# Gated linear attention and a routed two-layer network on one core: batches in pairs with both states in PSUM, padded tile loads, rows of x in 64x64 products, weights loaded later, steps in another order

## The chip, the cores and the metric

One core of a Trainium2 chip. The time is device microseconds of one launch. The core's engines run beside each other: TensorE (PE; the loading of its weights is shown as PEld), VectorE (DVE), ScalarE (ACT), GpSimd (POOL), and SyncE (SP), which here only starts transfers. 16 DMA engines carry all transfers.

## What is computed

Inputs q, k, v and alpha have 4 batches, 8 heads, 768 steps and 48 values per head. Per batch and head a 48x48 state runs through time:

```python
for t in range(S):
    state = alpha[:, :, t, :, None] * state + np.einsum('bhd,bhe->bhde', k[:, :, t], v[:, :, t])
    y[:, :, t] = np.einsum('bhd,bhde->bhe', q[:, :, t], state)
```

The result, as 3072 rows x of 384 values, goes into a routed network: rows with `x @ w_skip > 0` are computed, each by the one of 8 experts with the largest logit `x @ w_gate`:

```python
h = np.maximum(xc[mask] @ w1[e], 0.0)          # 384 -> 1024
y[mask] = gate_w[mask, None] * (h @ w2[e])     # 1024 -> 384
out[do_compute] = xc + y
```

All other rows are copied. Everything is fp32.

## The kernel before

**Tiles.** A tile i is 128 time steps of one batch with all 8 heads; there are 24 (`NT`). Heads lie in pairs, 48 of 64 partitions each. Tiles go through the four batches in turn: tiles 0 to 3 are the first 128 steps of batches 0 to 3, so that a batch comes back four tiles later, and each batch has its state in SBUF (`state`, four buffers).

**One tile.** `load` (L200) brings the decays, k and q (`qka`, 1551 columns) and v. Tiles 0 and 1 come from `first`, an array padded to 128 partitions, in three pieces; the later ones in two transfers of 48 partitions, moved by 16 partitions in odd tiles (`shift`), into one of six buffers that were filled with zeros at the start. `decay` (L215) makes running products of alpha: a forward scan `pfx` on DVE (L219) and a reciprocal, POOL multiplies q by it (L222); a backward scan `sfx` on DVE (L224), and POOL multiplies k by that (L226). PE then makes `scores` (L229) in 64x64 quadrants of its array, and DVE's `causal` (L240) copies their lower triangle out of PSUM. `turn_k` (L244) turns k with four full-array transposes, and ACT copies the result (`kt`, L252). The state: `held` (L256) puts the old state into PSUM with a product with the identity (L259), `outer` (L262) adds the products of k and v of the two halves of the tile (s = 0 and 1, L272) with a copy of the state between them (`half`, L276), and `carry` (L278) multiplies by the tile's total decay while it copies the state to SBUF (L281). y is summed in PSUM from `inter` (query times state) and `intra` (scores times v), both L290, and copied by `turn_y` (L328). One iteration later `rows` (L331) turns y into rows of x together with the logits, in four products (8 records) that use 112 of the 128 array rows and 105 columns (L335), into bank `pg`; `row_copy` (L341) takes x out on ACT, `logits` (L346) sums the logits on DVE, `store` writes the 128 rows to the output.

**Order.** All orders are written by hand in `static_path`: the queue of each engine is the order of the calls. In iteration i of the loop (L824 to L901): load(i+5), store(i-2), a quarter of a weight matrix, scores(i+1), causal(i+1), inter(i), outer(i,1), carry(i), intra(i,0), turn_k(i+2), rows(i-1), decay(i+3), intra(i,1), turn_y(i), held(i+1), outer(i+1,0), row_copy(i-1), logits(i-1). `tick` spreads the routing operations of finished groups of tiles (groups of 6, 6, 6, 3, 2, 1) over the iterations; `rank`, `place`, `one_hot` and `table` give each row its slot in its expert's list. `weight_splits` cuts the weights into a high part (ACT) and a remainder (POOL or DVE), a sixth of a matrix at a time. `follow` adds a wait by hand.

**Weights.** `weight_loads` (L502) goes through w1 and w2 of expert 0, then 1 and so on, four transfers of 384 KB per matrix, into three buffers. 16 of these transfers are issued in the loop (i = 3 to 14 and 19 to 22), the rest by `advance(loads, 4)` after each expert's `up` and after its `down`.

**End of the loop and experts.** After the loop the last tiles are routed and the rows of expert 0 are gathered by products (`late_rows`) into three PSUM banks `x0t`. Then, for each expert: `up` (L584), `turn` of the next expert's gathered rows, `down` (L606) and a scatter. `guard` loads alpha once more in eight pieces through one buffer and lets ACT look for values out of range, to take a slower general path if need be.

Of the kernel before, what the change touches and what calls it, by code (L numbers as in the profile page):

```python
# [29 lines left out]
NF = 2  # L30
N = B * S
# [16 lines left out]
RW = 2 * D + E + 1  # L48
GO = NP * RW
# [11 lines left out]
class Kernel:  # L61
    def __init__(self, ctx, tc, first, qka, v, w9, w1, w2, nat, w9n, out):
        self.ctx, self.tc, self.nc = ctx, tc, tc.nc
        self.qka, self.v, self.w9, self.w1, self.w2, self.out = qka, v, w9, w1, w2, out
        self.first, self.nat, self.w9n = first, nat, w9n
        self.scatters = {}

    @staticmethod
    def row(i):
        return i % B * S + i // B * P  # L70

    @staticmethod
    def shift(i):
        return 16 * (i % 2)
# [35 lines left out]
    def attention_pools(self, st):  # L110
# [10 lines left out]
        self.state = [fix.tile([P, NP, D], F32, name=f"state{b}") for b in range(B)]  # L121
# [7 lines left out]
    def early_constants(self):  # L129
        nc, const = self.nc, self.const  # L130
        zero = nc.const_aps.tensor(0.0, [P, 1], F32)
# [19 lines left out]
    def row_constants(self):  # L151
# [4 lines left out]
        for h in range(2):  # L156
            r = slice(64 * h, 64 * h + D)
            nc.sync.dma_start(out=self.xw[r, :, 2 * D:], in_=self.w9[h])
            nc.scalar.copy(out=self.xw[r, :, h * D:(h + 1) * D],
                           in_=self.ident[r, r].unsqueeze(1).to_broadcast([D, NP, D]))  # L160
# [19 lines left out]
    def slot_constants(self):  # L180
# [10 lines left out]
        nc.gpsimd.iota(iv[:, :, 0:1].rearrange("p (c b) w -> p c b w", b=B), pattern=[[P, C], [S, B], [0, 1]],  # L191
                       base=-OFF, channel_multiplier=0)
# [7 lines left out]
    def load(self, i):  # L200
        nc = self.nc
        t = self.qkab[i % NQ]
        if i < NF:
            for s in (slice(0, DEC), slice(KO, QO), slice(QO, QW)):
                nc.sync.dma_start(out=t[:, s], in_=self.first[i, :, s])
        else:
            for r in range(2):
                o = HP * r + self.shift(i)
                nc.sync.dma_start(out=t[o:o + D, :], in_=self.qka[i - NF, r])
# [3 lines left out]
                            kh=t[:, KO:QO].rearrange("p (a t) -> p a t", t=P))  # L213

    def decay(self, i, eng=None):  # L215
        nc, w = self.nc, self.work[i]
        dec = w["dec"]
        pfx = self.sc.tile([P, DEC + 1], F32, name="pfx", bufs=5)
        nc.vector.tensor_tensor_scan(pfx[:, 0:DEC], dec, self.floor.to_broadcast([P, DEC]), FLOOR, ALU.mult, ALU.max)  # L219
        nc.vector.reciprocal(dec[:, P + 1::SEG], pfx[:, P + 1::SEG])  # L220
        w["total"] = pfx.rearrange("p (a w) -> p a w", w=SEG)[:, :, P + 2:P + 3]
        nc.gpsimd.tensor_tensor(w["qh"], w["qh"], pfx.rearrange("p (a w) -> p a w", w=SEG)[:, :, 1:P + 1], ALU.mult)  # L222
# [33 lines left out]
    def held(self, i):  # L256
        if i >= NT or i < B:
            return
        self.nc.tensor.matmul(self.pv[:, 0:NP * D], lhsT=self.ident, rhs=self.state[i % B].rearrange("p a d -> p (a d)"),  # L259
                              start=True, stop=True, skip_group_check=True)  # L260

    def outer(self, i, s):  # L262
        if i >= NT or (s == 1 and i // B == C - 1):
            return
        w = self.work[i]
        t = slice(HP * s, HP * (s + 1))
        pv = self.pv[:, 0:NP * D].rearrange("p (a d) -> p a d", d=D)
        for p in range(NP):
            for r in range(2):
                h = 2 * p + (r ^ p % 2)  # L270
                a = slice(HP * r, HP * (r + 1))
                self.nc.tensor.matmul(pv[a, p, :], lhsT=w["kt"][t, p, a], rhs=w["v"][t, h * D:(h + 1) * D],  # L272
                                      start=(i < B and s == 0 and p == 0), stop=True, skip_group_check=True)
# [4 lines left out]
    def carry(self, i):  # L278
        if i // B == C - 1:
            return  # L280
# [745 lines left out]
```

## Time and profile before

| | us |
|---|---|
| median of 3 runs | 336.9 |
| lowest and highest run | 336.19, 338.39 |
| the profiled execution | 336.32 |
| its span, first to last instruction | 334.5 |

PE is busy 286.5 us of the span, DVE 191.8, POOL 190.2, ACT 149.0. The attention loop ends at about 166 us of the span, the experts begin at about 182. Busy times overlap; a stage's bound is read from what waits for what in it. Records of PE are passes: an fp32 product shows as two records.

### The profile page before, as it was taken

The page shows a single profiled execution, that of the slowest core. Times are in us where ns is not written, and L with a number is a line of the kernel's source. Part 1 is how long each engine was busy: PE and PEld are TensorE (multiplying, and loading weights), DVE is VectorE, ACT ScalarE, POOL GpSimd, SP SyncE. Part 2 cuts the span into 40 slices and gives each one's busy share as a digit, 9 for nine tenths or more (in the row PEclk, how much of TensorE's full clock was granted, in tenths as well). Part 3 has the DMA queues.
Part 4 walks back from the last instruction along what each step waited for, and adds up shares of the span by engine and source line. Part 5 has one row for each costly group of instructions (what it writes and reads, how often), then busy time and mean ns, then how long its engine had stood idle before and what let it go on. Part 6 is the DMA issues. An engine that isn't in the chain of part 4 may idle for free.

```text
span 334.5 us, 10415 instructions
## 1 busy us (share of the span) xinstructions
PE 286.5 (86%) x4384; PEld 267.7 (80%) x4384; DVE 191.8 (57%) x368; ACT 149.0 (45%) x300; POOL 190.2 (57%) x208
## 2 busy tenths in 40 slices
PE   1767998787999888988897699998979899999991
PEld 1557987676878786877797599998979799999991
DVE  7564667683377846775054823819367386656540
ACT  6112233331234432352313636939396795555410
POOL 4543373373577749581495675746646487655521
PEclk9965699996599979998569979999999999999997
DMA  7999699989799985234110174958859496842100
GB/s 245 189 191 220 164 238 278 238 174 205 193 289 248 264 185 152 74 97 122 53 48 4 43 256 159 361 174 294 299 209 328 148 340 221 292 131 92 34 21 23
DMA packets 25495, 61.01 MB, mean 182 GB/s; under 512 B 4118, under 2 KB 11183, under 8 KB 25440
## 3 DMA queue, kind: packets, MB, share of 16 engines
q1 hardware_dynamic: 23264, 55.22, 58.8%
q0 software_dynamic: 2176, 5.05, 4.4%
q8 instruction: 36, 0.59, 0.8%
q14 instruction: 19, 0.16, 0.2%
HBM read 52.63 MB, written 8.85 MB: 184 GB/s over the span
## 4 chain that ended last, share of the span: by engine, by line
PE 53%; DMA 11%; ACT 11%; issue 9%; DVE 8%; POOL 5%; SPq 2%; POOLq 0%; ACTq 0%; DVEq 0%
PE ps_o L615 10%; PE ps_h L599 9%; PE ps_y L290 8%; DMA alpha<-in_nat_dram 8%; PE ps_g L335 6%; PE ps_v L272 6%; ACT over L568 4%; PE ps_k L250 3%; PE ps_v L259 3%; PE ps_s L237 3%; DMA qka<-in_qka_dram 3%; ACT w2h L531 2%; POOL qka L226 2%; DVE pfx L219 2%; SPq L511 1%
## 5 line engine op out<-in xcount | busy, mean ns | idle before, releaser
L222 POOL TENSOR_TENSOR qka<-qka,pfx 128x512 f32<-128x512 f32 x24 | 26.2, 1092 | 53.4 <-DVE pfx L219 17.6
L615 PE MATMUL ps_o<-w2h,hh 128*112 128x384 f32 (+1 forms) x128 | 44.2, 346 | 0.0
L615 PE MATMUL ps_o<-w2l,hh 128*112 128x384 f32 (+1 forms) x128 | 43.9, 343 | 0.0
L615 PE MATMUL ps_o<-w2h,hl 128*112 128x384 f32 (+1 forms) x128 | 43.7, 341 | 0.0
L535 POOL TENSOR_TENSOR w2l<-raw,w2h 128x512 fp32r<-128x512 f32 x18 | 24.2, 1346 | 28.3 <-ACT w2h L531 28.3
L272 PEld LDWEIGHTS ps_v<-vt,kt 64*64 64x64 f32 x704 | 30.7, 162 | 11.0 <-issue 7.9
L272 PE MATMUL ps_v<-vt,kt 64*64 64x48 f32 x704 | 35.4, 247 | 4.4 <-issue 3.7
L599 PE MATMUL ps_h<-xh,w1h 128*128 128x240 f32 x192 | 32.9, 277 | 6.4 <-DVE hl L604 4.8
L252 ACT COPY kt<-ps_k 128x512 f32<-128x512 f32 x24 | 14.0, 584 | 49.6 <-PE ps_k L250 49.6
L604 DVE SCALAR_TENSOR_TENSOR hl<-ps_h,hh 128x480 fp32r<-128x480 f32 x32 | 20.8, 650 | 26.3 <-ACT hh L603 26.2
L535 POOL TENSOR_TENSOR w1l<-raw,w1h 128x512 fp32r<-128x512 f32 x24 | 31.4, 1310 | 4.5 <-ACT w1h L531 4.3
L226 POOL TENSOR_TENSOR qka<-qka,sfx 128x512 f32<-128x512 f32 x23 | 29.3, 1273 | 7.6 <-DVE sfx L224 6.7
L290 PE MATMUL ps_y<-st,vt 64*48 64x64 f32 x768 | 29.6, 250 | 4.6 <-issue 3.5
L599 PEld LDWEIGHTS ps_h<-xh,w1h 128*128 128x128 f32 x192 | 27.3, 190 | 7.2 <-DVE hl L604 5.3
L620 POOL DMA_INDIRECT out_dram<-o,ids x16 | 18.7, 1168 | 24.4 <-DVE o L618 22.2
L219 DVE TENSOR_TENSOR_SCAN pfx<-qka,ps_c 128x527 f32<-128x527 f32 x24 | 29.8, 1240 | 4.6 <-DMA qka<-in_qka_dram 3.8
L599 PE MATMUL ps_h<-xh,w1l 128*128 128x240 f32 x192 | 32.4, 275 | 0.0
L237 PE MATMUL ps_s<-qka 64*64 64x64 f32 x768 | 22.9, 255 | 10.6 <-DVE qka L226 7.2
L599 PE MATMUL ps_h<-xl,w1h 128*128 128x240 f32 x192 | 31.7, 274 | 0.0
L224 DVE TENSOR_TENSOR_SCAN sfx<-qka,ps_c 128x525 f32<-128x525 f32 x24 | 29.9, 1247 | 2.7 <-POOL slots L198 0.5
L568 ACT ACTIVATE over<-alpha,lim 128x1152 bf16<-128x1152 f32 x16 | 20.2, 1264 | 24.0 <-DMA alpha<-in_nat_dram 23.7
L453 POOL DMA_INDIRECT xr<-out_dram,ids x18 | 21.2, 1178 | 14.5 <-DVE gate L385 8.7
(139 smaller groups left out, 666.1 us busy)
## 6 DMA issues: line engine op xcount, KB each, us to landing
raw<-in_w_dram SPq DMA_DIRECT2D x64, 384.0 KB
qka<-in_qka_dram SPq DMA_DIRECT2D x44, 290.8 KB
vt<-in_v_dram SPq DMA_DIRECT2D x24, 192.0 KB
out_dram<-x SPq DMA_DIRECT2D x24, 192.0 KB
alpha<-in_nat_dram SPq DMA_DIRECT2D x8, 576.0 KB
out_dram<-xr SPq DMA_DIRECT2D x6, 192.0 KB
qka<-in_first_dram SPq DMA_DIRECT2D x4, 256.0 KB
qka<-in_first_dram SPq DMA_DIRECT2D x2, 263.5 KB
```

Source lines behind the costliest of these rows:

```text
L219: nc.vector.tensor_tensor_scan(pfx[:, 0:DEC], dec, self.floor.to_broadcast([P, DEC]), FLOOR, ALU.mult, ALU.max)
L222: nc.gpsimd.tensor_tensor(w["qh"], w["qh"], pfx.rearrange("p (a w) -> p a w", w=SEG)[:, :, 1:P + 1], ALU.mult)
L224: nc.vector.tensor_tensor_scan(sfx[:, 2:DEC][:, ::-1], dec[:, 2:DEC][:, ::-1], self.floor.to_broadcast([P, DEC - 2]), FLOOR, ALU.mult, ALU ...
L226: (eng or nc.gpsimd).tensor_tensor(w["kh"], w["kh"], sfx.rearrange("p (a w) -> p a w", w=SEG)[:, :, 2:P + 2], ALU.mult)
L237: self.nc.tensor.matmul(self.ps[t, r, p * HP:(p + 1) * HP], lhsT=kh[a, p, t], rhs=qh[a, p, t], start=True, stop=True, skip_group_check=True)
L272: self.nc.tensor.matmul(pv[a, p, :], lhsT=w["kt"][t, p, a], rhs=w["v"][t, h * D:(h + 1) * D], start=(i < B and s == 0 and p == 0), stop=Tr ...
L290: return self.nc.tensor.matmul(self.py[HP * c:HP * c + D, p % 2, o:o + HP], lhsT=lhsT, rhs=rhs, start=first, stop=True, skip_group_check=True)
L453: return [self.nc.gpsimd.indirect_dma_start(out=xr[:n, j, :], out_offset=None, in_=self.out[:, :], in_offset=bass.IndirectOffsetOnAxis(ap= ...
L535: eng.tensor_tensor(lo[:, s], raw[:, s], hi[:, s].bitcast(F32), ALU.subtract)
L568: nc.scalar.activation(out=over, in_=a, func=AF.Relu, scale=scale, bias=self.lim[:, j:j + 1], accum_out=self.odd[:, j, g:g + 1])
L599: nc.tensor.matmul(ps[:, u, :], lhsT=a[:, k, f * P:(f + 1) * P], rhs=b[:, k, :], start=(n == 0), stop=(n == len(order) - 1))
L615: nc.tensor.matmul(ps[:r], lhsT=a[:, f, js], rhs=b[:, f, :], start=(n == 0), stop=(n == 3 * FT - 1))
```

## The change

- **Pairs.** Tiles go through two batches at a time (`G = 2`): tiles 0 to 11 are batches 0 and 1, tiles 12 to 23 batches 2 and 3. Both states stay in one PSUM bank (`region`). `held` is gone; `carry` multiplies in place in PSUM; a new `keep` lets ACT copy the state to SBUF for the next `inter`. `outer` waits for the last `carry`.
- **Loads.** All tiles are padded to 128 partitions on the host and loaded in one transfer (tiles 0 and 1 in three pieces, as before). The zero fills, `first` and `shift` are gone. Tile 5 is loaded before the loop, ahead of the small loads of `xw`.
- **Rows.** `rows` makes 16 products per tile in 64x64 quadrants, 48 rows by 57 columns, into the two banks of the scores, columns 256 on; `row_copy` and `logits` read these two banks.
- **Order.** `decay` is called in two parts: the forward scan after `carry`, the backward scan after `row_copy` and `logits`, which now follow `rows` at once. `outer(i+1, 0)` comes before `intra(i, 1)`.
- **Weights.** 12 quarters are issued in the loop, one each at i = 5, 8, 10, 12 and two each at i = 18 to 21; splits start at i = 10 instead of 6. The late clears move from i = 10..15 to i = 15..20.

```diff
+G = 2
-RW = 2 * D + E + 1
-GO = NP * RW
+RW = D + E + 1
+RO = NP * HP
+GO = 0
...
+    def chunk(i):
+        return i % (G * C) // G
...
     def row(i):
-        return i % B * S + i // B * P
+        return (i // (G * C) * G + i % G) * S + Kernel.chunk(i) * P
...
-        nc.vector.memset(self.qkab[2], 0.0)
-        for i in range(3, 5):
-            nc.scalar.copy(out=self.qkab[i], in_=zero.to_broadcast([P, QW]))
...
     def load(self, i):
-        if i < NF:
-            for s in (slice(0, DEC), slice(KO, QO), slice(QO, QW)):
-                nc.sync.dma_start(out=t[:, s], in_=self.first[i, :, s])
-        else:
-            for r in range(2):
-                o = HP * r + self.shift(i)
-                nc.sync.dma_start(out=t[o:o + D, :], in_=self.qka[i - NF, r])
+        for s in (slice(0, DEC), slice(KO, QO), slice(QO, QW)) if i < NF else (slice(0, QW),):
+            nc.sync.dma_start(out=t[:, s], in_=self.qka[i, :, s])
...
-    def held(self, i):
-        if i >= NT or i < B:
-            return
-        self.nc.tensor.matmul(self.pv[:, 0:NP * D], lhsT=self.ident, rhs=self.state[i % B].rearrange("p a d -> p (a d)"),
-                              start=True, stop=True, skip_group_check=True)
...
     def outer(self, i, s):
-        pv = self.pv[:, 0:NP * D].rearrange("p (a d) -> p a d", d=D)
+        pv = self.region[i % G]
...
+                if s == p == r == 0 and self.carried:
+                    self.follow(ins.ins, self.carried)
...
     def carry(self, i):
-        self.nc.vector.tensor_tensor(self.state[i % B], self.pv[:, 0:NP * D].rearrange("p (a d) -> p a d", d=D),
-                                     self.work[i]["total"].to_broadcast([P, NP, D]), ALU.mult)
+        pv = self.region[i % G]
+        ins = self.nc.vector.tensor_tensor(pv, pv, self.work[i]["total"].to_broadcast([P, NP, D]), ALU.mult)
+        self.carried = ins.ins.name
+
+    def keep(self, i):
+        self.nc.scalar.copy(out=self.state[i % G], in_=self.region[i % G])
...
     def rows(self, i):
         for p in range(NP):
-            self.nc.tensor.matmul(bank[:, p * RW:(p + 1) * RW], lhsT=w["xt"][:PD, p, :], rhs=self.xw[:PD, p, :],
-                                  start=True, stop=True, skip_group_check=True)
+            for s in range(2):
+                for c in range(2):
+                    a = slice(HP * c, HP * c + D)
+                    t = slice(HP * s, HP * (s + 1))
+                    self.nc.tensor.matmul(self.ps[t, c, RO + p * RW:RO + (p + 1) * RW], lhsT=w["xt"][a, p, t],
+                                          rhs=self.xw[a, p, :], start=True, stop=True, skip_group_check=True)
...
-            for i in range(1, 5):
+            for i in range(1, 6):
                 self.load(i)
...
-                if i + 5 < NT:
+                if 0 < i < NT - 5:
                     self.load(i + 5)
...
-                if 3 <= i < 15 or 19 <= i < 23:
+                if i in (5, 8, 10, 12):
                     advance(loads)
-                if 10 <= i < 16:
-                    self.clear_late(i + 8)
+                if 18 <= i < 22:
+                    advance(loads, 2)
+                if 15 <= i < 21:
+                    self.clear_late(i + 3)
...
                 self.carry(i)
-                tick(2)
+                tick(1)
+                if i + 3 < NT:
+                    self.decay(i + 3, 0)
                 self.intra(i, 0)
...
                 if i:
                     self.rows(i - 1)
+                    self.row_copy(i - 1)
+                    self.logits(i - 1)
                 if i + 3 < NT:
-                    self.decay(i + 3)
+                    self.decay(i + 3, 1)
+                if not last:
+                    self.outer(i + 1, 0)
                 self.intra(i, 1)
                 self.turn_y(i)
+                self.keep(i)
                 if last:
                     break
-                self.held(i + 1)
-                self.outer(i + 1, 0)
-                if i:
-                    self.row_copy(i - 1)
-                    self.logits(i - 1)
...
-                if 6 <= i < 18:
+                if 10 <= i < 22:
                     advance(splits)
...
-            self.x0t = [self.ps[:, 0, 0:ROOM], self.ps[:, 1, 0:ROOM], self.pk[:, 0:ROOM]]
+            self.x0t = [self.pk[:, 0:ROOM], self.pv[:, 0:ROOM], self.py[:, 0, 0:ROOM]]
```

## Rows read from the trace of the kernel before

**Rows 1.** Busy time by stretch; the first line names the columns.
```profile
core 0: us, PE busy (x) PEld busy (x) DVE busy (x) ACT busy (x) POOL busy (x), PEclk, DMA share, GB/s
...
4.00:9.00 5.00, 1.78 (x36) 1.69 (x36) 4.54 (x7) 2.18 (x4) 1.94 (x3) 1.00 1.07 318
...
20.00:30.00 10.00, 9.47 (x206) 8.86 (x199) 5.14 (x8) 3.24 (x8) 4.88 (x8) 0.50 1.07 200
40.00:75.00 35.00, 29.91 (x866) 26.34 (x864) 25.84 (x49) 13.18 (x29) 19.45 (x30) 1.00 0.95 233
77.40:91.10 13.70, 13.26 (x272) 11.55 (x268) 4.97 (x10) 3.67 (x8) 5.55 (x6) 0.51 0.78 176
```

**Rows 2.** ACT's order of time: start, us, then the copy in `turn_y`, L328.
```profile
20.49 0.58 ACT L328 COPY xt<-ps_y 112x512 f32<-112x512 f32 x1 [0.80 <-PE ps_y L290]
...
41.77 0.58 ACT L328 COPY xt<-ps_y 112x512 f32<-112x512 f32 x1 [0.74 <-PE ps_y L290]
...
166.09 0.58 ACT L328 COPY xt<-ps_y 112x512 f32<-112x512 f32 x1 [2.32 <-PE ps_y L290]
```

**Rows 3.** Chain that ended last, 40 to 62 us: start, us, what.
```profile
39.82 0.59 PE ps_k L250 x4
...
42.77 0.42 PE ps_s L237 x25
...
44.36 0.59 PE ps_k L250 x4
44.95 0.87 PE ps_g L335 x8
...
46.20 0.52 PE ps_v L259 x2
```

**Rows 4.** The same chain, its longest pieces over the whole span.
```profile
5.04 9.13 DMA qka<-in_qka_dram
...
17.09 1.28 POOL qka L226
18.41 0.67 PE ps_k L250 x4
...
74.68 2.50 issue
...
79.82 0.77 PE ps_s L237 x28
...
84.59 1.67 PE ps_g L335 x8
...
86.87 0.94 PE ps_v L259 x2
...
88.83 0.77 PE ps_s L237 x28
```

**Rows 5.** Waits of the whole span: us in total, times, longest us.
```profile
DVE ps_c L346 <- ACT x L341: 42.9, 22, 4.9
...
ACT over L568 <- DMA alpha<-in_nat_dram: 23.7, 4, 8.6
...
PE ps_y L290 <- issue: 6.1, 7, 2.5
...
PE ps_h L599 <- DVE hl L604: 4.8, 3, 2.0
...
PE ps_v L272 <- issue: 3.7, 2, 1.9
...
PE ps_s L237 <- issue: 3.4, 2, 2.3
```

**Rows 6.** Groups by line: count, busy us, mean ns, idle before.
```profile
L224 DVE TENSOR_TENSOR_SCAN sfx<-qka,ps_c 128x525 f32<-128x525 f32 x24 | 29.9, 1247 | 2.7 <-POOL slots L198 0.5
...
L341 ACT COPY x<-ps_g 128x384 f32<-128x384 f32 x23 | 11.2, 485 | 0.0
...
L346 DVE TENSOR_REDUCE ps_c<-ps_g 128x9 f32<-128x36 f32 x23 | 4.7, 204 | 43.1 <-ACT x L341 42.9
```

More of the change, by code (lines that the diff above doesn't have):

```diff
@@ L120, in attention_pools @@
         self.stb = [fix.tile([P, 2, NP * HP], F32, name=f"st{i}") for i in range(2)]
-        self.state = [fix.tile([P, NP, D], F32, name=f"state{b}") for b in range(B)]
+        self.state = [fix.tile([P, NP, D], F32, name=f"state{b}") for b in range(G)]
+        self.region = [self.pv[:, b * NP * D:(b + 1) * NP * D].rearrange("p (a d) -> p a d", d=D) for b in range(G)]
         self.xtb = [fix.tile([P, NP, P], F32, name=f"xt{i}") for i in range(2)]
@@ L157, in row_constants @@
             r = slice(64 * h, 64 * h + D)
-            nc.sync.dma_start(out=self.xw[r, :, 2 * D:], in_=self.w9[h])
-            nc.scalar.copy(out=self.xw[r, :, h * D:(h + 1) * D],
+            nc.sync.dma_start(out=self.xw[r, :, D:], in_=self.w9[h])
+            nc.scalar.copy(out=self.xw[r, :, 0:D],
                            in_=self.ident[r, r].unsqueeze(1).to_broadcast([D, NP, D]))
@@ L212, in load, with decay @@
         self.work[i] = dict(dec=t[:, 0:DEC], v=vt, qh=t[:, QO:QW].rearrange("p (a t) -> p a t", t=P),
-                            kh=t[:, KO:QO].rearrange("p (a t) -> p a t", t=P))
-    def decay(self, i, eng=None):
+                            kh=t[:, KO:QO].rearrange("p (a t) -> p a t", t=P), begun=set())
+    def decay(self, i, part, eng=None):
         nc, w = self.nc, self.work[i]
         dec = w["dec"]
[L218 to L222, printed above, removed]
+        if part == 0:
+            pfx = self.sc.tile([P, DEC + 1], F32, name="pfx", bufs=5)
+            nc.vector.tensor_tensor_scan(pfx[:, 0:DEC], dec, self.floor.to_broadcast([P, DEC]), FLOOR, ALU.mult,
+                                         ALU.max)
+            nc.vector.reciprocal(dec[:, P + 1::SEG], pfx[:, P + 1::SEG])
+            w["total"] = pfx.rearrange("p (a w) -> p a w", w=SEG)[:, :, P + 2:P + 3]
+            nc.gpsimd.tensor_tensor(w["qh"], w["qh"], pfx.rearrange("p (a w) -> p a w", w=SEG)[:, :, 1:P + 1],
+                                    ALU.mult)
+            return
         sfx = self.sc.tile([P, DEC + 1], F32, name="sfx")
@@ L295, in inter @@
         for s in range(2):
-            if not s and i < B:
+            if not s and self.chunk(i) == 0:
                 continue
-            src = w["half"] if s else self.state[i % B]
+            src = w["half"] if s else self.state[i % G]
             for p in range(NP):
@@ L913, in static_path @@
             self.late_split(a)
-            self.rows(b, bank=self.pv)
-            self.logits(b, bank=self.pv)
-            self.row_copy(b, bank=self.pv)
+            self.rows(b)
+            self.logits(b)
+            self.row_copy(b)
             last = self.route(groups[5], nc.vector)
@@ L970, in static_path @@
                 advance(loads, 4)
-NAMES = ("first", "qka", "v", "w9", "w1", "w2", "nat", "w9n")
+NAMES = ("qka", "v", "w9", "w1", "w2", "nat", "w9n")
 def kernel_body(tc, *args):
@@ L993, in layouts @@
     flat = lambda a: a.reshape(NT, 2, D, -1)
-    qka = np.concatenate([flat(decay)[..., :DEC], flat(heads(k)), flat(heads(q))], axis=3)
-    first = np.zeros((NF, P, QW), qka.dtype)
-    for i in range(NF):
-        for r in range(2):
-            o = HP * r + Kernel.shift(i)
-            first[i, o:o + D] = qka[i, r]
-    qka = qka[NF:]
-    vt = v.reshape(B, H, C, P, D).transpose(2, 0, 3, 1, 4).reshape(NT, P, DM)
+    qka = np.zeros((NT, 2, HP, QW), alpha.dtype)
+    qka[:, :, :D] = np.concatenate([flat(decay)[..., :DEC], flat(heads(k)), flat(heads(q))], axis=3)
+    qka = qka.reshape(NT, P, QW)
+    vt = tiles(v).transpose(0, 2, 1, 3).reshape(NT, P, DM)
     w9 = np.concatenate([moe_w_gate, moe_w_skip[:, None]], axis=1).reshape(NP, 2, D, E + 1).transpose(1, 2, 0, 3)
@@ L1007, in layouts @@
     w2 = moe_w2.reshape(E, FT, P, DM).transpose(0, 2, 1, 3).reshape(E, P, FT * DM)
-    return [np.ascontiguousarray(a) for a in (first, qka, vt, w9, w1, w2, nat, w9n)]
+    return [np.ascontiguousarray(a) for a in (qka, vt, w9, w1, w2, nat, w9n)]
 def kernel(**inputs):
```

63 lines of the change are left out of this document (31 added, 32 removed).

## The prediction

> **What bounds the kernel now.** I read first the table by stretch of time, then the chain of work that ended last, then groups by line, then the waits. TensorE (PE) is the engine that is nearly always busy, at two clock levels: 0.50 of full speed in 20 to 30 us, 1.00 in 40 to 75 us, 0.51 in 77.4 to 91.1 us [rows 1]. The attention loop has 24 iterations, one per tile; the copy of the finished tile (`turn_y`, L328) marks each: tile 0 at 20.49, tile 3 at 41.77, tile 23 at 166.09 [rows 2]. So the 20 iterations after tile 3 take 124.3 us, 6.2 each. How long is a clean one? In the chain at full clock, one `turn_k` starts at 39.82 and the next at 44.36: 4.54 us, all PE [rows 3]. At the lower level the scores start at 79.82 and again at 88.83: 9.01 us [rows 4]. The rest of 124.3: 20 x 4.54 = 90.8; "issue" waits of PE 13.2 in eleven [rows 5], of which some 10.8 fall here, the longest 2.50 [rows 4]; about three low-clock iterations at 4.47 extra, 13.4; what is left, 9.3, I put on routing work. DMA shows a busy share of 1.07 in 20 to 30 us and 0.95 in 40 to 75 us [rows 1].
>
> **Part 1, state kept in PSUM.** `held` goes: an identity product of 2 records in 20 tiles, 0.52 us at full clock [rows 3], 0.94 at the lower [rows 4], all on PE's chain. `carry` stays one VectorE (DVE) operation of the same shape, now written to PSUM; `keep` adds an ACT copy of 192 columns, under the 0.485 us of the 384-column copy [rows 6], on an engine that is busy 13.2 of 35 us [rows 1]. Hidden by that; uncovered it would be 20 x 0.49 = 9.8 us at most. The new wait, `outer(i+1,0)` behind `carry(i)`, has `intra`, `turn_k` and `rows` in front of it on PE, over 1.1 us [rows 3]; cost between 0 and the length of a late carry; I take 0.
>
> **Part 2, rows of x in quadrants.** 8 records become 32. At full clock the 8 take 0.87 us [rows 3]. Score products have the same quadrant form: 25 records in 0.42 us, 16.8 ns each [rows 3], so 32 take 0.54: -0.33. At the lower level 1.67 becomes 32 x 0.77/28 = 0.88: -0.79 [rows 4]. The bounds are 0 (no gain) and these. With part 1, PE needs 4.54 - 0.52 - 0.33 = 3.69 us per clean iteration, and 9.01 - 0.94 - 0.79 = 7.28 at the lower level.
> The Trainium skill (TensorE: Matmul & The Clock Gate, "Wait — 56ns, not 53.3ns?") states that start to start never falls below about 25 ns. By that the rows would take 0.80, an estimate, and the sum below would end 5 us later; the trace's 16.8 ns differs, and it decides here.
>
> **Part 3, the order of steps.** This puts the gain of PE in doubt. `decay` is cut: its forward scan comes right after `carry`, its backward scan behind `row_copy` and `logits` of tile i-1. So a ring closes: `turn_k(i+2)` 0.59, `rows` 0.54, row copy 0.49, `logits` 0.20, backward scan 1.25, POOL's product for k 1.28, then `turn_k(i+3)` [rows 3, 4, 6]. The hand-off from POOL to PE took 0.04 (17.09 + 1.28 to 18.41 [rows 4]); for five I allow 0.25. Sum 4.60. PE has 0.9 us to spare per iteration, and 4.6, not 3.69, is the pace at full clock. At the lower level PE's 7.28 is the longer.
> `logits` waited for the row copy 22 times, 42.9 us [rows 5]: two readers of one bank follow each other. The Trainium skill (PSUM — Partial Sum Buffer, Terms) has it as a rule that two engines must not read one bank at once; the trace agrees. If the new layout let them overlap, the ring would be 4.1 and the sum 10 us less.
> The rows now lie in the banks of the scores, so `scores(i+2)` also waits for that copy and sum. These end about 0.7 us after `rows`, beside `outer` and `intra`; I take 0, with 0.5 per iteration as the other end.
>
> **Part 4, one padded load per tile.** 596 KB in two transfers of 48 partitions become 794 KB over 128. Which rate? In 4 to 9 us, when the padded tiles 0 and 1 were loaded over 128 partitions, DMA moved 318 GB/s; in 20 to 30 us, with 48-partition loads, 200 GB/s at a full busy share [rows 1]. So 2.5 us per tile at the one rate and 4.0 at the other, against 3.0 now. I take 2.5, the row of the same shape. Tile 2 sets the start: PE's `turn_k(2)` waits until 18.41 for a chain that begins with its load, a DMA piece of 9.13 us to 14.17 [rows 4]. 1.98 MB before it and its 0.794 MB at 318 GB/s are 8.7 us, from about 2: 10.7, and 3.3 us (rounded) come off the start (at 200 GB/s it is 1.0 later). The zero fills that go stood beside DMA waits: 0. The small load of `xw` is moved behind tile 5: 5.9 MB ahead of it, 18.7 us at 318 GB/s, so it lands near 21, when `rows(0)` is due near 20; with its latency I charge 2 us (0 to 12).
>
> **Part 5, weights later.** 12 quarters rather than 16 are loaded in the loop, 4 of them before iteration 13; the first split moves four iterations later, and its POOL products lie beside PE as now. In the expert stage each matrix is loaded one place later. ScalarE waits there four times for the guard's alpha, 23.7 us, and PE three times behind it, 4.8 us [rows 5]: now SP stands before a weight load until the splits free a buffer, and alpha is behind it. After the change the first load finds a free buffer and alpha g0 comes early; later ones trade places with loads that land just in time. Bounds -4.8 and, one matrix of 1.57 MB late at 233 GB/s [rows 1], +7. I take -1.5. The last tile's rows at the end of the loop, at the lower level, give -0.8.
>
> **Sum.** Start -3.3. Iterations 1 to 3 have no `held` now: rows 3 x 0.79 = -2.4 against `xw` +2, so about 0. The 20 iterations: 20 x 4.60 = 92.0; issue waits, those parts over PE's 0.9 spare: 5; low clock in 2.5 iterations x (7.28 - 4.60) = 6.7; routing 8 of 9.3, as a little is covered by the spare: 111.7 against 124.3, -12.6. With -0.8 and -1.5: -18.2. The profiled execution took 336.3 us (its span 334.5 and 1.8 around it): 318.1. The median shown is 336.9, 0.2% above; 318 is my time for either.
>
> **Rivals.**
> 1. The split `decay` costs more: POOL also makes one-hots and weight remainders between two k products, and if they stand in front of it the ring is 5.2, 20 x 0.6 = +12: 330. For: every link of the ring is a wait. Against: POOL is busy only 19.5 of 35 us [rows 1].
> 2. The padded third is paid at today's rate. After the first tiles 27.9 MB must move before tile 23 can be scanned (22 tiles of 0.991, 18 stores and 5 clears of 0.197, 4 weight quarters of 0.39). At 200 GB/s 140 us: tile 23 lands near 148; it is scanned in iteration 20, so some 3.4 iterations of 6.2 are left and the loop ends at 169: +3, less 2.3 of tail and experts: 337. From 235 GB/s on it lands before 128 and is hidden. For: 200 is the rate of unmixed tile loads. Against: their 48 partitions.
> 3. Slower: the clock. PE's full-array work (`held`, 128-wide `rows`) gives way to small products and idle time in the ring; if PE then runs at its lower level for 12 of the 20 iterations rather than 2.5, 9.5 x 2.68 = +25: 343. It decides from 9 iterations on (then nothing is gained). For: at 0.51 PE stayed 13.7 us though busy 13.3 of them. Against: at 29.9 busy of 35 us it kept 1.00 [rows 1].
> 4. The expert stage loses all three waits and the low-clock stretches vanish: -3.3 and -5 more, 310.
>
> **Chances.** Forecast 0.62 (309 to 327), rival 1 0.14, rival 2 0.07, rival 3 0.07, rival 4 0.10. A measurement tells about 1%, 3.4 us, from no change. Faster by over 1%: forecast and rivals 1 and 4, 0.86; within: rival 2, 0.07; slower: rival 3, 0.07. The range 303 to 332 leaves out rivals 2 and 3 and a little at either end.
>
> **What would show it.** Tile 2's forward scan before 11.5 us; DMA over 260 GB/s in 5 to 20 us; clean iterations of 4.5 to 4.8 with a short PE wait for POOL's k product; 32 records of rows in under 0.6 us; granted clock 1.00 in most of 40 to 140 us; `turn_y` of tile 23 near 149; the expert stage within 2 us of before. Wrong if iterations stay above 5.5 at full clock, if the scans wait for loads in the loop, or if the clock is low in half of it.

## The result: 4.9% faster, with most of the gain at the start

The changed kernel took 323.07 us (median of 4 runs, 318.52 to 324.42) beside 337.64 us for the kernel before on the same chip (4 runs, 336.19 to 346.26): a ratio of 0.951, 95% interval 0.935 to 0.967. The forecast was 318.0 with a range of 303 to 332. The profiled execution took 324.42 us, its span 322.6. Executions of one kernel differ by 2 to 3% (of the changed kernel the profiled one is the slowest of four), so ratios and their intervals leave out runs more than 1.5% above the fastest of the same kernel, and below a single profile is used for what repeats in it, and medians for totals.

**Stage by stage.** The table by stretch of time of the kernel before, cut at `turn_y` of tiles 0, 3 and 23 and at the first product of the experts, which comes at 178.16 and not, as said above, at about 182 (columns as in [rows 1]):

```profile
20.49:41.77 21.28, 18.90 (x373) 17.60 (x370) 10.99 (x18) 5.73 (x13) 7.32 (x11) 0.55 0.88 191
41.77:166.09 124.32, 108.48 (x2780) 94.75 (x2779) 76.76 (x170) 42.80 (x99) 72.83 (x94) 0.89 0.74 189
166.09:178.16 12.07, 9.61 (x61) 9.13 (x61) 5.84 (x31) 3.20 (x8) 11.61 (x13) 0.73 0.11 37
178.16:334.50 156.34, 141.08 (x1016) 139.15 (x1016) 83.99 (x133) 89.86 (x171) 87.73 (x75) 0.97 0.53 183
```

The same of the changed kernel:

```profile
17.69:31.88 14.19, 12.24 (x474) 10.73 (x466) 10.22 (x18) 6.84 (x17) 7.47 (x10) 1.00 0.83 274
31.88:157.94 126.06, 101.14 (x3172) 89.79 (x3172) 77.34 (x170) 47.68 (x116) 73.91 (x95) 0.80 0.66 210
157.94:168.53 10.59, 8.51 (x85) 8.21 (x85) 5.74 (x31) 2.82 (x8) 10.10 (x12) 0.75 0.11 40
168.53:322.60 154.07, 141.80 (x1016) 139.92 (x1016) 83.02 (x133) 91.18 (x171) 88.35 (x75) 0.97 0.54 186
```

| part | predicted | measured (span) |
|---|---|---|
| up to `turn_y` of tile 0 | -3.3 | 20.49 to 17.69: -2.8 |
| iterations 1 to 3 | 0 | 21.28 to 14.19: -7.1 |
| the 20 iterations after tile 3 | -12.6 | 124.32 to 126.06: +1.7 |
| from there to the experts | -0.8 | 12.07 to 10.59: -1.5 |
| experts | -1.5 | 156.34 to 154.07: -2.3 |
| sum | -18.2 | -11.9 |

So the total came out near the forecast by two errors of opposite sign. PE does 7.3 us less in the 20 iterations (108.48 to 101.14), and they are no shorter: its mean granted clock there fell from 0.89 to 0.80. A second profile of the changed kernel (experiment 5) has the same pattern with a smaller error in the loop: -3.2, -6.6, -4.8, -0.4 and -1.8, in sum -16.8. So the loop gained 0 to 5 us of the 12.6 forecast.

**What turned out as said.** The chain of work around tile 2, which answers to [rows 4] (start, us, what):

```profile
4.56 6.31 DMA qka<-in_qka_dram
...
10.89 1.26 DVE pfx L216
...
13.72 1.29 POOL qka L226
...
15.06 1.11 PE ps_k L250 x4
```

The load's piece is 6.31 us where it was 9.13, and the forward scan starts at 10.89 (forecast 10.7). The waits, which answer to [rows 5]: five of PE in the 20 iterations, then two of the expert stage:

```profile
PE ps_y L292 <- issue: 5.8, 4, 2.1
PE ps_g L436 <- POOL hot L424: 5.4, 11, 0.7
PE ps_v L266 <- issue: 4.0, 3, 2.4
PE ps_k L250 <- POOL qka L226: 3.1, 6, 1.2
PE ps_s L340 <- issue: 2.1, 2, 1.9
...
ACT over L572 <- DMA alpha<-in_nat_dram: 9.7, 3, 3.4
...
PE ps_h L603 <- DVE hl L608: 2.8, 2, 1.8
```

ScalarE's alpha waits are 9.7 us instead of 23.7, PE's behind it 2.8 instead of 4.8.

**Where the loop's gain is.** The table by stretch again, of the changed kernel: DMA at the start, a clean iteration, the first two of six in which the table of slots is made, then one PE stall and the stretch behind it:

```profile
9.00:20.00 11.00, 10.21 (x218) 8.81 (x216) 8.35 (x12) 3.20 (x7) 6.39 (x6) 1.00 1.03 395
49.42:53.92 4.50, 3.43 (x133) 2.87 (x132) 3.18 (x9) 2.13 (x6) 2.05 (x2) 1.00 0.66 193
...
72.41:80.34 7.93, 5.35 (x170) 4.79 (x174) 3.89 (x6) 2.49 (x6) 4.63 (x5) 0.85 0.72 255
80.34:87.28 6.94, 5.80 (x164) 5.19 (x161) 3.94 (x8) 1.98 (x5) 5.37 (x5) 0.75 0.69 226
106.00:108.50 2.50, 0.14 (x7) 0.07 (x3) 1.00 (x4) 0.00 (x0) 2.35 (x2) 1.00 0.90 274
109.00:115.00 6.00, 6.00 (x159) 5.43 (x155) 3.93 (x6) 2.71 (x6) 2.10 (x2) 0.50 0.42 150
```

Clean iterations take 4.5 us (4.41 to 4.50 in iterations 1, 3, 7 and 10), as the ring of part 3 said (4.60). The six iterations 11 to 13 and 17 to 19 take 7.93, 6.94, 6.97, 6.75, 6.19 and 6.96. The chain shows what stands in them:

```profile
72.48 1.25 DVE sfx L224
73.73 0.62 DVE st L242
74.35 0.73 DVE pfx L216
75.08 0.47 POOL mv L429
75.56 1.83 POOL hot L424 x2
...
77.43 0.51 PE ps_g L436 x3
77.94 1.03 PE ps_s L340 x32
```

POOL makes two one-hots (1.83 us) behind the k product; PE's `table` waits for them; `rows` is behind `table` on PE; the row copy, the logits and the next backward scan are behind `rows`. So the one-hots are a link of the ring. Before, `logits` stood behind `decay(i+3)` in DVE's queue, and PE waited 1.7 us for one-hots in the 20 iterations. And the last two rows of the table above show the second effect: PE stands for 2.36 us with nothing that the profile names ("issue"), and in the next stretch it is busy 6.00 of 6.00 us at 0.50. In this profile each low stretch from 30 us to 150 us begins within 1.7 us of the end of a stall of PE of 0.6 us or more; six other stalls of that length are followed by none.

### The profile page after: what moved, and what is told of

Its sections match the earlier page's. It is cut to its first block, busy times and chain, and to the rows that moved or that the text cites. A ratio compares the mean times of both kernels' runs of the same rounds, so it can differ in the third digit from the quotient of the medians.

```text
span 322.6 us, 11454 instructions
## 1 busy us (share of the span) xinstructions
PE 273.5 (85%) x4920; PEld 256.9 (80%) x4920; DVE 189.7 (59%) x367; ACT 153.5 (48%) x318; POOL 189.3 (59%) x208
## 4 chain that ended last, share of the span: by engine, by line
PE 54%; issue 11%; DMA 10%; DVE 8%; ACT 7%; POOL 7%; SPq 1%; POOLq 0%; DVEq 0%; ACTq 0%
PE ps_o L619 14%; PE ps_h L603 13%; PE ps_y L292 7%; PE ps_s L340 5%; DMA raw<-in_w_dram 4%; PE ps_v L266 4%; PE ps_s L237 3%; ACT over L572 3%; PE ps_k L250 3%; POOL hot L424 3%; DVE sfx L224 3%; DMA alpha<-in_nat_dram 3%; ACT x L345 2%; DMA qka<-in_qka_dram 2%; PE ps_g L436 2%
## 5 line engine op out<-in xcount | busy, mean ns | idle before, releaser
L266 PE MATMUL ps_v<-vt,kt 64*64 64x48 f32 x704 | 36.1, 250 | 4.7 <-issue 4.0
L292 PE MATMUL ps_y<-st,vt 64*48 64x64 f32 x768 | 36.1, 257 | 3.9 <-issue 3.9
L252 ACT COPY kt<-ps_k 128x512 f32<-128x512 f32 x24 | 14.1, 586 | 53.1 <-PE ps_k L250 53.1
L266 PEld LDWEIGHTS ps_v<-vt,kt 64*64 64x64 f32 x704 | 32.3, 168 | 5.7 <-issue 4.6
L607 ACT ACTIVATE hh<-ps_h 128x480 fp32r<-128x480 f32 x32 | 18.3, 571 | 31.0 <-PE ps_h L603 27.0
L292 PEld LDWEIGHTS ps_y<-st,vt 64*48 64x48 f32 x768 | 27.7, 146 | 4.4 <-issue 4.4
```

The lines of the kernel that those rows point to most:

```text
L266: ins = self.nc.tensor.matmul(pv[a, p, :], lhsT=w["kt"][t, p, a], rhs=w["v"][t, h * D:(h + 1) * D], start=(i % (G * C) == s == p == 0), st ...
L292: return self.nc.tensor.matmul(self.py[HP * c:HP * c + D, p % 2, o:o + HP], lhsT=lhsT, rhs=rhs, start=first, stop=True, skip_group_check=True)
```

## The experiments

**Theory A**: the loop's gain is held up by one-hots in the ring and by PE's stalls, each of which also brings half clock behind it. **Rivals**: small products themselves bring the half clock, or it comes whatever the order (B); a bound in DMA or PE's work. Kernel n is the kernel of experiment n. Experiments 1 to 4 stand beside the kernel before at 335.14 us (15 runs).

**1. The table behind intra(i,1).** Where the six calls stood:

```diff
-                    if g[0] < 12 and i in (g[1] + 5, g[1] + 6, g[1] + 7):
...
-                        self.table((n, n + 1))
...
                 self.intra(i, 1)
+                for g in groups[:2]:
+                    if i in (g[1] + 5, g[1] + 6, g[1] + 7):
...
+                        self.table((n, n + 1))
```

> Edit: in the changed kernel, the call of table moves from before rows to behind intra(i,1) on PE. Theory A (the one-hots of POOL and the table product stand in the ring that the split decay closed: k product, one-hots, table, rows, row copy, logits, backward scan, k product): the six iterations with a table (11 to 13 and 17 to 19), 6.96 us each on average in the changed kernel, fall to about 5.2, so 10 us less: 312 to 314. Theory B (these iterations are slow because POOL has too much to do in them, or because the clock is low): POOL's work and the clock are as before, so they stay above 6.5 and the time at 320 or more.

319.11 us (4 runs, 311.75 to 321.78), short of theory A's 312 to 314. Iterations 11 and 12, by stretch of time:

```profile
71.18:76.22 5.04, 3.80 (x150) 3.22 (x150) 3.40 (x5) 2.42 (x6) 3.64 (x5) 1.00 0.92 316
76.22:81.29 5.07, 4.30 (x154) 3.85 (x153) 3.84 (x8) 1.92 (x6) 4.61 (x5) 1.00 0.75 259
```

7.93 and 6.94 became 5.04 and 5.07, 17 and 18 became 5.14 and 4.21. That the one-hots lengthened these iterations through the ring is shown in these four; 13 and 19 became longer (8.36 and 9.00). The 20 iterations took 118.44: iterations 13, 14, 16, 19 and 20 now had issue waits (15.2 us in 13 over the 20 iterations) or low clock or both and took 7.5 to 9.0.

**2. Both scans together behind carry**, so that no ring through `rows` is left:

```diff
                 if i + 3 < NT:
                     self.decay(i + 3, 0)
+                    self.decay(i + 3, 1)
...
-                if i + 3 < NT:
-                    self.decay(i + 3, 1)
```

> Edit: in the changed kernel, both parts of decay are called behind carry, so that the backward scan no longer waits for logits. Theory A (ring through rows, copy, logits and backward scan): that ring is gone, table iterations fall by some 1.5 us, 6 x 1.5 = 9; but logits now stand behind both scans on DVE, and scores(i+2), in the same banks, behind logits: a new ring of about 5.0 us in place of 4.5 in the clean iterations, 14 x 0.5 = +7. Together 319 to 323, with clean iterations at 5.0. Theory B (no ring counts): clean iterations stay at 4.4 to 4.5, and the time at 323 within 2.

319.99 us (6 runs; ratio 0.952, 0.935 to 0.968), in theory A's range, the 20 iterations 121.80 at 0.81. The longest of PE's waits in them:

```profile
PE ps_s L237 <- DVE ps_c L350: 14.6, 13, 2.1
```

Waits for one-hots shrank from 5.4 to 1.5 us, and a new one came: the scores share their banks with the rows of x, so `scores` waits for `logits`, which now stand behind 2.5 us of scans. This cost, which part 2 put at 0 with 0.5 per iteration as its other end, is real as soon as the logits are late.

**3. Two loads of 48 partitions per tile**, with the zero fills, as before the change:

```diff
...
+            for r in range(2):
+                o = slice(HP * r, HP * r + D)
+                nc.sync.dma_start(out=t[o, :], in_=self.qka[i, o, :])
```

> Edit: in the changed kernel, tiles 2 and on are loaded in two transfers of 48 partitions without the padding rows, and their buffers are zero-filled once. Theory A (the rate follows from how many partitions a load covers): 200 to 240 GB/s in the stretch 9 to 20 us in place of 395, the first forward scan of tile 2 at 14 us in place of 10.9, turn_y of tile 0 3 us later, and busy DMA through the loop: 326 to 333. Theory B (the bytes count): a quarter fewer bytes of tiles, tile 2 no later than 10.9, the time 323 or less.

331.76 us (10 runs; ratio 0.990, 0.982 to 0.997), as theory A said: against the changed kernel's 323.07 and 320.33 (below, on another chip) the padded loads are worth 8.7 and 11.4 us. By stretch of time:

```profile
9.00:20.00 11.00, 8.31 (x164) 6.91 (x166) 7.61 (x10) 2.74 (x6) 6.27 (x6) 1.00 1.04 219
19.65:39.80 20.15, 13.79 (x474) 12.26 (x466) 10.28 (x17) 6.94 (x17) 7.52 (x10) 0.83 0.89 198
```

At the same busy share, 219 GB/s over 48 partitions against 395 over 128. The size of a transfer doesn't explain it: the 48-partition ones are 291 KB, and tiles 0 and 1, in pieces of 256 and 264 KB over 128 partitions, came at 318 GB/s [rows 1]. Tile 0 ends 2.0 us later and iterations 1 to 3 take 20.15 instead of 14.19 us. So most of the 7 us that I had not forecast are the loads too; 3.0 us of them are one wait of PE for `xw`, which lands later behind slower loads.

**4. Rows as four full-array products in their old bank**, the rest of the change kept:

```diff
...
-                    self.nc.tensor.matmul(self.ps[t, c, RO + p * RW:RO + (p + 1) * RW], lhsT=w["xt"][a, p, t],
-                                          rhs=self.xw[a, p, :], start=True, stop=True, skip_group_check=True)
+            self.nc.tensor.matmul(self.pg[:, p * RW:(p + 1) * RW], lhsT=w["xt"][:PD, p, :], rhs=self.xw[:PD, p, :],
+                                  start=True, stop=True, skip_group_check=True)
```

> Edit: in the changed kernel, rows goes back to four full-array products per tile in a bank of their own. Theory A (idle time of PE in the ring lets the clock fall): mean granted clock in the loop stays near 0.80; rows cost 0.2 more at full clock and 0.6 more at the lower, all in the ring: 326 to 330. Theory B (small products in place of full-array work let the clock fall): mean clock in the loop back near 0.89, and the time at 322 or less.

318.59 us (4 runs; ratio 0.957, 0.945 to 0.970): no loss, as theory B said. Iterations 4 to 8 in one stretch, then the 20 iterations:

```profile
33.15:58.37 25.22, 20.83 (x712) 18.90 (x708) 19.93 (x40) 11.07 (x27) 15.13 (x26) 1.00 0.80 258
33.15:149.79 116.64, 96.10 (x2682) 86.28 (x2674) 76.27 (x171) 47.71 (x115) 73.31 (x94) 0.89 0.69 223
```

A clean iteration takes 5.04 instead of 4.5, yet the 20 take 116.64, with one issue wait of 1.5 us and a clock of 0.89. In these profiles the small rows save PE work and give it back in stalls and low clock. Whether that is their number (490 records more in the 20 iterations) or their kind no run settles (the last section has a reading that speaks for the number): the six profiles with full-array rows (4 and 6 to 10) have issue waits of 1.5 to 8.0 us there, the seven with small rows 8.7 to 15.2, but the kernel before, with few records too, had 10.9.

**5. The changed kernel again, and two parts undone.** On another chip, before 336.74 us (17 runs). As it is:

> The changed kernel as it is, on the chip of the three runs beside it. Both theories: a median of 319 to 325 us, a span near 322, the 20 iterations after tile 3 in 122 to 127 us, and in them PE's issue waits of 8 to 15 us and three to six iterations over 6 us where the table waits for POOL's one-hots.

320.33 us (6 runs, 316.85 to 323.10; ratio 0.963, 0.944 to 0.982); the 20 iterations, 119.53 us, are under the 122 to 127 expected. Part 1 undone (`held` ahead of `outer(i+1,0)`, one `region` for both batches, `keep` gone):

```diff
-        ins = self.nc.vector.tensor_tensor(pv, pv, self.work[i]["total"].to_broadcast([P, NP, D]), ALU.mult)
+        ins = self.nc.vector.tensor_tensor(self.state[i % G], pv, self.work[i]["total"].to_broadcast([P, NP, D]), ALU.mult)
...
+                    self.held(i + 1)
                     self.outer(i + 1, 0)
```

> Undoes part 1 alone: the state goes back to SBUF and comes into PSUM by an identity product ahead of outer(i+1,0); keep goes. Theory A (the ring through DVE and POOL sets the clean iterations, so PE has about 0.5 us to spare): at full clock nothing, at the lower level 0.94 for each such iteration: 0 to +9 us, about +4, and a granted clock in the 20 iterations within 0.03 of 0.80. Theory B (PE is the bound all along): 20 x 0.52 to 0.94, +10 to +14 us. Theory C (PE loses its clock for want of full-array work, and the identity products give some of it back): granted clock 0.85 or more and no time lost, or some gained.

331.79 us (6 runs, 324.63 to 334.30; ratio 0.986, 0.948 to 1.025). Iteration 10 and the 20 iterations of each, as it is and with `held`:

```profile
67.47:71.67 4.20, 3.22 (x141) 2.62 (x131) 3.18 (x7) 2.12 (x5) 2.37 (x2) 1.00 0.77 220
...
32.02:151.55 119.53, 96.36 (x3172) 85.96 (x3172) 77.42 (x170) 47.39 (x115) 73.86 (x95) 0.83 0.68 217
```

```profile
70.76:75.37 4.61, 4.17 (x161) 3.37 (x156) 3.12 (x7) 1.90 (x6) 2.37 (x2) 1.00 0.70 217
...
34.15:161.93 127.78, 106.34 (x3196) 90.53 (x3188) 78.55 (x169) 44.10 (x99) 73.58 (x94) 0.85 0.62 203
```

PE has 10.0 us more to do and the stretch is 8.3 longer. In the order by pairs 17 such products fall in it, not the 20 of my expectation: 9 to 16 us by theory B. The 8.3 lies just below that and inside theory A's 0 to 9, and the two profiles of the changed kernel differ by 6.5 us there, so the stretches alone don't part the two. The runs speak for B: all six are above all six of the kernel as it is, by 11.5 us at the median. So do iterations 3 and 10, at full clock in both traces: 4.36 and 4.20 us as it is, 5.12 and 4.61 with `held`, so the ring did not hide the product even there. Theory C falls: time is lost at a clock of 0.85.

Part 5 undone:

```diff
-                if i in (5, 8, 10, 12):
+                if 3 <= i < 15 or 19 <= i < 23:
                     advance(loads)
-                if 18 <= i < 22:
-                    advance(loads, 2)
...
-                if 10 <= i < 22:
+                if 6 <= i < 18:
                     advance(splits)
```

> Undoes part 5 alone: weight quarters are loaded in iterations 3 to 14 and 19 to 22, the splits run in iterations 6 to 17. Theory A (part 5 is worth what the expert stage shows): ScalarE's waits for the guard's alpha go back from 9.7 to over 20 us, and the expert stage becomes 1 to 3 us longer, the loop within 2 us. Theory B (the loop suffers from DMA traffic and from POOL's remainders, and later weights spare it): the 20 iterations after tile 3 become 4 us or more longer.

329.63 us (12 runs, 326.45 to 332.09; ratio 0.993, 0.984 to 1.002). Waits in its expert stage:

```profile
ACT over L572 <- DMA alpha<-in_nat_dram: 25.1, 4, 8.4
...
PE ps_h L603 <- DVE hl L608: 6.9, 3, 3.0
```

The alpha waits are back, PE's behind them 6.9 us against 2.8, and the experts take 160.0 us against 154.5; the loop 121.3 against 119.5. By the medians part 5 is worth 9 us, by the profiles 6.9, of which 5.5 lie in the expert stage, the place that I had named; the 1 to 3 us said for it is missed. That stage varies, from 151.5 to 158.0 us in the twelve profiles that have part 5, and it took 156.3 before. What repeats is the wait for alpha: 9.2 to 10.5 us in all twelve, 23.7 and 25.1 in the two without.

**6. Rows full, both scans together, table behind intra(i,1)**: edits 1, 2 and 4 in one.

> The changed kernel with three edits together: rows as four full-array products in their old bank, both scans of the decay right behind carry, the table behind the last intra products. Theory A (the 20 iterations are long because of the ring, the one-hots in it and the issue waits of the small products): no ring is left, clean iterations at 3.9 to 4.6 us, issue waits under 5 us, granted clock 0.88 or more, the 20 iterations in 104 to 113 us, the time 306 to 315 us. Theory B (PE's clock and POOL's load set the loop, whatever the order): the 20 iterations stay at 116 us or more, the time at 317 to 324 us.

315.61 us (6 runs, 311.46 to 320.09; ratio 0.945, 0.928 to 0.962). The time lies between the two ranges (0.6 above A's), the loop in B's: clean iterations of 3.94 to 4.53, but 118.88 us for the 20, at 0.81, with 8.0 us of issue waits. One of these, of 1.87 us, ended at 46.78, and the iteration behind it (47.33 to 54.61) ran at 0.52.

**7. A stall added.** Kernel 4 with one more POOL product ahead of the k product in iterations 4 and 15:

```diff
+        if i in (7, 18):
+            nc.gpsimd.tensor_tensor(self.dummy, w["kh"], sfx.rearrange("p (a w) -> p a w", w=SEG)[:, :, 2:P + 2], ALU.mult)
         (eng or nc.gpsimd).tensor_tensor(w["kh"], w["kh"], sfx.rearrange("p (a w) -> p a w", w=SEG)[:, :, 2:P + 2],
```

> The kernel with rows as four full-array products (its iterations 4 to 8 and 16 took 5.03 to 5.05 us each at granted clock 1.00), with one more POOL product of 128x512, about 1.28 us, put ahead of the k product in iterations 4 and 15, so that turn_k of the next iteration comes late. Theory A (a stall of PE is followed by a stretch at half clock, and that is what the stalls really cost): within about 3 us of each added stall the granted clock falls to 0.50 for 3 us or more, and the two iterations behind the stall take 10.1 + 1.3 + at least 1.5 us. Theory B (the clock falls for other reasons): clock 1.00 there, the iteration takes 5.05 + 1.3 and the next 5.05 again.

One run, 327.52 us. Kernel 4 without the stall, iterations 5 and 6, and 16 and 17:

```profile
38.20:48.28 10.08, 8.33 (x292) 7.55 (x288) 7.55 (x13) 4.34 (x11) 5.65 (x5) 1.00 0.89 299
102.61:115.10 12.49, 9.40 (x293) 8.29 (x287) 7.94 (x15) 4.88 (x12) 8.16 (x8) 0.97 0.74 238
```

With it, the same iterations, the stall itself and the stretch behind it:

```profile
38.16:51.37 13.21, 10.99 (x293) 10.24 (x288) 7.67 (x13) 4.36 (x11) 6.66 (x6) 0.74 0.69 231
107.59:121.25 13.66, 10.59 (x298) 9.59 (x293) 7.88 (x15) 4.88 (x13) 9.44 (x9) 0.88 0.67 221
...
40.15:42.07 1.92, 0.00 (x0) 0.00 (x0) 1.59 (x3) 0.00 (x0) 1.84 (x3) 0.84 0.71 174
42.50:48.50 6.00, 6.00 (x125) 5.72 (x127) 2.19 (x3) 2.19 (x5) 1.85 (x2) 0.52 0.52 190
```

The first added product of 1.28 us made PE stand for 1.92 us, the granted clock went to its lower level and stayed there for about 7 us, and the two iterations took 3.1 us longer: the stall's own 1.3 and 1.8 for the clock, as theory A said. At the second place they took 1.2 us longer. There the lower level came 1.7 us behind the stall, for 3.4 us, but kernel 4 has such a stretch of its own nearly at the same point, so this place decides nothing. That a stall of PE brings half clock behind it is shown by one added stall, and the traces together bear it out: of 34 stalls of PE of 1.8 us or more that came at full clock between 25 and 150 us, 31 have the lower level begin during the stall or within 2 us behind it. It isn't so each time: in kernel 9 below PE stood for 1.89 us until 62.42, and 62.5 to 68.5 was granted 1.00.

**8. The table in the next iteration**, ahead of `turn_k`, in kernel 6:

> The combined kernel (rows as full-array products, both scans behind carry) with the table put into the next iteration, ahead of turn_k, so that neither the one-hots nor the logits are late for it. Theory A (what still costs in the combined kernel is PE's stalls and the half clock behind them; two of its eight stalls of over 0.6 us in 30 to 148 us stood before the table): no PE wait over 0.3 us for one-hots or logits, 20 iterations 3 to 8 us shorter than the combined kernel's 118.9, so 111 to 116, a time of 308 to 315 us. Theory B (the half-clock stretches come whatever the order): the 20 iterations within 2 us of 118.9, a time of 314 to 319 us.

325.07 us (6 runs; ratio 0.975, 0.968 to 0.982): slower than kernel 6, outside both theories' times. The edit has a fault: `table_add` came to stand behind the two scans on DVE, and `rows`, whose bank it reads, waited for it:

```profile
PE ps_g L336 <- DVE tab L443: 8.2, 4, 2.2
```

Yet its 20 iterations took 117.88 us in the profile, as theory B said and no longer than kernel 6's 118.88, so it isn't settled that this wait makes the difference of the medians.

**9. The early one-hots on VectorE** in kernel 4, ring and table left where they are:

```diff
-                            self.one_hot(t, nc.gpsimd)
+                            self.one_hot(t, nc.vector)
```

> The kernel with rows as four full-array products, and the early one-hots made by VectorE (0.35 us each where it makes them today) in place of POOL (0.93 us). Everything else stays, the ring too. Theory A (POOL's one-hots stand in the ring through the k product and hold the table up, and the half clock follows these stalls): iterations 11 to 13 and 17 to 19, which took 6.2 to 9.1 us, come to 5.0 to 5.4 us each unless an issue wait falls in them, no PE wait for one-hots is left, the 20 iterations take 103 to 110 us against 116.6, the time is 306 to 313 us. Theory B (half-clock stretches come as often whatever the order): the 20 iterations at 114 us or more, the time at 316 to 322 us.

315.87 us (6 runs, 313.23 to 321.40) beside 336.81 (11 runs; ratio 0.938, 0.930 to 0.946). The 20 iterations, then iteration 19:

```profile
32.94:144.28 111.34, 89.88 (x2682) 80.97 (x2674) 84.73 (x183) 47.55 (x115) 62.91 (x82) 0.95 0.74 235
...
116.90:122.41 5.51, 4.62 (x157) 4.23 (x152) 5.44 (x12) 2.69 (x7) 1.88 (x2) 1.00 0.86 278
```

PE's 5.7 us of waits for one-hots are gone, five of the six iterations take 5.5 to 5.9 us (the sixth, 8.05, holds a stall of 1.98), and the mean clock is 0.95. Theory A's waits are gone as it said, its ranges missed by 1.3 and 2.9 us; theory B's are missed too, the time by 0.1. The higher clock can't be laid to the edit: over the whole span kernel 4 had 0.918 in its profiled run and 0.949 to 0.955 in its other three, kernel 9 0.928 to 0.954 in its six.

**10. The same with both scans behind carry**: no ring and no one-hots on POOL.

> The same with both scans of the decay right behind carry, so that no ring is left; the table stays ahead of rows. Theory A: clean iterations near PE's own 4.2 to 4.5 us, in iterations 11 to 13 and 17 to 19 too; with stalls for issue of 3 to 8 us and the half clock behind them the 20 iterations take 97 to 107 us, the time is 302 to 311 us. Theory B (with less waiting PE falls to half clock more, so that nothing is won over the kernel with the ring): the 20 iterations within 3 us of that kernel's, the time at 313 us or more.

311.99 us (6 runs, 309.67 to 313.33; ratio 0.930, 0.924 to 0.935). All its runs are below all runs of the changed kernel (those of experiment 5 on another chip), and its median is 3.9 us below kernel 9's on the same chip. The 20 iterations:

```profile
32.49:140.37 107.88, 89.87 (x2682) 81.02 (x2674) 85.23 (x184) 47.44 (x116) 63.07 (x83) 0.95 0.75 239
```

18.2 us less than in the changed kernel's first profile and 11.7 less than in its second, with PE's rows in their old, slower form. Theory A's ranges (97 to 107 and 302 to 311) are missed by 1 us each, B's by 0.5 and 1.0 on the other side. This is the best version found.

## Why the prediction was right in the total and wrong in its steps

- **The bound before** was read rightly (PE, two clock levels), but low stretches were only counted there, not traced to the stalls ahead of them. [rows 4] had the 2.50 us wait ending at 77.18, and [rows 1] the level of 0.51 from 77.4: the two stood side by side.
- **Part 1.** I took `held` off PE (0.52 and 0.94 per product), then let the ring hide most of it. Experiment 5 has it worth 8 us in the loop and 11.5 by the medians: the ring did not hide it.
- **Part 2.** 32 records took 0.62 to 0.66 us at full clock (forecast 0.54) and 1.05 at the lower level (0.88; before 0.87 and 1.67): 19 to 21 ns each at full clock. The Trainium skill (TensorE: Matmul & The Clock Gate, "Wait — 56ns, not 53.3ns?") has 25 ns as the least; the traces stay below it. The shared banks cost little in the change's own order (1.4 us of `scores` behind `logits`), and 14.6 us in experiment 2.
- **Part 3.** The ring was right (4.60; 4.2 to 4.5 in clean iterations). What failed is the step "routing 8 of 9.3" in the sum: I let the pace hold for all 20 iterations, and gave one-hots in the ring a chance of 0.14 as rival 1, at 0.6 us per iteration. They cost in six iterations only, but 41.7 us in place of 6 x 4.60 = 27.6: 14.1 us (16.7 in the second profile) where 8 was put. Part of that is half clock behind the stalls. The other fourteen iterations took 19.9 us over 14 x 4.60, where 5 for issue waits and 6.7 for the clock were put; the two excesses, 6.1 and 8.2, are the distance between 111.7 and 126.06. In the second profile the fourteen took 10.8 over, about what was put, so the routing step is the one that is off in both. The second term that was mis-sized is the clock: 2.5 iterations or 18 us at the lower level by the forecast, and at a mean of 0.80 about 0.40 x 126.06 = 50 us in the profile (0.34 x 119.53 = 41 in the second). Rival 3 had this, and laid it to small products and to idle time of PE in the ring: experiment 7 bears out the idle time. The small products aren't settled: full-array `held` in experiment 5 hardly raised the clock (0.83 to 0.85), and the profiles with full-array rows range from 0.81 to 0.95.
- **Part 4.** The rate was right, even low (318 taken, 395 reached). Its worth was not: I counted the start (-3.3; -2.8 measured) and nothing in iterations 1 to 3, where before the granted clock was 0.55 and after 1.00. Experiment 3 puts 6 us there. Of the 2 us charged for `xw`, none came up in the first profile and 0.4 us in the second; experiment 3, with slower loads, waited 3.0 us for it. Two slips stand in the working of part 4: 14.17 less 10.7 is 3.5, not 3.3, and at 200 GB/s the tile would land 1.7 later, not 1.0; neither moves the forecast by more than 0.2.
- **Part 5.** -1.5 by forecast, -2.3 in the profile, and 5.5 us of experts when it is undone, which is outside the bound of -4.8. The shorter wait for alpha is shown, its worth in time is not, as that stage varies by more.
- **The total.** Two errors of about 7 and 14 us with opposite signs left 323 where 318 was said: that the total came so near is luck. `turn_y` of tile 23, said for 149, came at 157.94, and at 151.55 in the second profile.

## What to carry to other kernels

When an edit makes a step wait for the result of the step before it (here the scan behind the logits), list all that stands ahead of each link on its engine in *any* iteration, the rare ones too: a short job on a slow engine becomes a link. And where a trace shows TensorE at two clock levels, price a stall of TensorE as the stall plus a part of the low stretch behind it (1.8 of 6.8 us in experiment 7, up to half where TensorE has no slack): look for what ends just before each low stretch, and remove that, before making TensorE's work smaller.

## What the runs showed of the hardware

**Stalls and the clock.** A PE stall of 1.92 us was followed by about 7 us at 0.50, of 2.36 us by over 6 us; one of 1.89 us, and one of 2.26 us in the kernel before, by none. The Trainium skill (TensorE: Matmul & The Clock Gate, "HAM oscillation — how this bites in real kernels") describes one kernel in which TensorE waits some 3 to 5 us for a transfer ahead of each tile, and each tile begins at the lower level. These traces agree in the direction, with shorter stalls, and experiment 7 by an added one.

**One-hots on VectorE beside POOL.** One takes 0.35 us there when POOL rests, and up to 1.37 beside a POOL product (0.92 on POOL). DVE and POOL in order of time, kernel 10:

```profile
75.66 0.61 DVE L420 TENSOR_SCALAR hot<-slots,s 128x256 fp32r<-128x256 f32 x2
...
108.19 2.56 DVE L420 TENSOR_SCALAR hot<-slots,s 128x256 fp32r<-128x256 f32 x2
```

```profile
108.06 1.28 POOL L226 TENSOR_TENSOR qka<-qka,sfx 128x512 f32<-128x512 f32 x1 [0.41 <-DVE sfx L224]
109.28 1.32 POOL L535 TENSOR_TENSOR w1l<-raw,w1h 128x512 fp32r<-128x512 f32 x1
```

Two took 0.61 us while POOL had nothing, and 2.56 beside two POOL products of 1.28 and 1.32, ending 0.15 us after the second of these. The Trainium skill (SBUF — State Buffer, "SBUF: two separate sides") has the two engines share a pair of ports, for some operations of DVE, under an exclusive lock that makes the loser wait for the whole instruction; the rows agree. My 0.35 us came from six one-hots made when POOL has little to do; in experiment 9 DVE was busy 5.44 of 5.51 us in iteration 19, so it, not PE, was near its limit there.

**Issue waits.** No row of the instructions names their cause, but the DMA queues of the changed kernel's trace have one of another kind (queue, kind: packets, MB, share of 16 engines):

```profile
q8 instruction: 40, 0.66, 0.8%
```

Its packets are 16 KB each. In the 20 iterations 26 of them came in the changed kernel, 21 in kernel 4 and 22 in the kernel before, about one for every 250 records of PE and PEld (6385, 5379 and 5587). In all fourteen traces, of the 90 issue waits of PE of 0.5 us or more between 20 and 160 us, 88 end 1.2 to 1.75 us after such a packet has landed; of PE's 185 other waits of that length 17 do. So an issue wait reads as PE standing for its next block of instructions, and smaller products, being more records, need more blocks. That is argued from the timing; no run changed it alone.

**Left open.** Why some blocks come late and most in time. It also wasn't tried whether POOL's weight remainders could be kept out of the one-hot iterations.
